# A fused linear-attention and MLP block: value products ahead of the key products, and a new hand-written order

## The chip, the cores and the metric

The kernel runs on one core of a Trainium2 chip. The core has a matrix engine (PE, with its own weight loads, PEld), a vector engine (DVE), a scalar engine for activations (ACT), GpSimd (POOL) and SyncE (SP), which only issues DMAs here. The metric is the device time in microseconds (us). A time is the median of some runs; one further execution was recorded by the profiler, and all views of the profile come from it.

## The reference, cut to what matters

```python
def _A_ref(x, wqkv, w_phi, wo):              # S = 2048 tokens, D = 640, H = 32 heads of 20
    q, k, v = split(x @ wqkv)
    pq = einsum("bhsd,hdf->bhsf", q, w_phi)
    pk = einsum("bhsd,hdf->bhsf", k, w_phi)
    phi_q = concat([softmax(pq), softmax(-pq)])      # over the 20 features of a head
    phi_k = concat([softmax(pk), softmax(-pk)])
    kv = einsum("bhsf,bhsd->bhfd", phi_k, v)
    z  = einsum("bhsf->bhf", phi_k)
    num = einsum("bhqf,bhfd->bhqd", phi_q, kv)
    den = einsum("bhqf,bhf->bhq", phi_q, z)[..., None] + 1e-6
    return (num / den) merged over heads @ wo
def _B_ref(x, w1, w2):                       # 640 -> 1728 -> 640
    return silu(x @ w1) @ w2

h  = x + _A_ref(layernorm(x), wqkv, w_phi, wo)
h2 = h + _B_ref(layernorm(h), w1, w2)
```

## The kernel before, in words

The 2048 tokens are 16 tiles of 128. Everything but the inputs and the result stays on the chip. The products accumulate in `mm`, which is the whole accumulator memory: eight banks of 128 x 512 f32.

The program is a list of words, `ORDER`. Each word calls a function `op_<name>` with the numbers behind the dots, and `@n` names the bank of `mm` that it starts in. Each engine carries out its own instructions in the order of the words, and waits by semaphores for what its operands and its bank need. No scheduler moves anything. A letter at a word's end picks the engine: `v` is DVE, `a` is ACT, `p` is POOL, `s` is SP (`q` and `b` split a tile between POOL and DVE). The words that matter here:

- Loads: `lx.a.b` tiles a to b of x (160 KB a tile), `lk.a.b` and `lv.a.b` pieces of the key weights wk and the value weights wv (160 KB for each 128 rows, five in all), `lp` w_phi, `lq.c` a part of the query weights, transposed by the DMA into the memory of wk, `lo`, `l1`, `l2`, `lh` the later weights.
- Layernorm of a tile t: `st.t` statistics on DVE (L267, L268), `rs` the reciprocal root (L272 on DVE for one tile, then a power on POOL, L275), `xn.t` the normalised tile (L291 on DVE, L296 on ACT). It is transposed by PE (`xt.t`, L302, five matmuls against the identity, and a copy `xc.t`) or by the DMA (`xd.t`, L309).
- Key weights folded with w_phi, so that one product gives pk: `wt.c` transposes a chunk of wk on PE (L316), `wc.c` copies it out (L166 or L168), `ph` multiplies w_phi by a mask that `mk` makes (L195), `fk.c` is the fold (L331, six matmuls) and `fc.c` copies it into Wfk. `gk` and `gc` do the same for the query weights.
- Products of a tile, ten matmuls of 128 x 320 (L364): `kp.t` with Wfk, `vp.t` with wv. `vc.t` copies v out of the accumulator.
- phi_k of a tile: `ke.t` the exponentials on ACT (L389), `kr.t` sums and reciprocals on DVE (L397, L400), `kn.t` the division on POOL (L407; with `q` or `b` DVE does a part, L411). `cc.t` adds the tile to kv (L420, 32 small matmuls).
- When kv is complete, `kc` and `km` bring it into the form for the queries. `mt` (with `mc`, a mask) prepares that.
- Queries, by groups of four tiles: `qp.g.i` products (L451), `qe.g.i` exponentials. Then for each tile `dp.t` multiplies with kv (L486, 40 small matmuls over four banks), `dw.t` and `dr.t` form num / den on DVE (L500 to L515), `do.t` finishes it on POOL or DVE (L521), `td.t` transposes by DMA, `op.t` is the product with wo (L548), `oa.t` adds x on DVE (L557).
- The MLP: `sq`, `sr`, `hn`, `hd` the second layernorm, `up.g.k` products with w1 (L627, L637), `ua` silu, `yp` and `yh` products with w2 (L673, L686), `yo` and `yz` the last addition and the store.
- `wm.n` is a dummy matmul of n columns on constants (L262) whose result nobody reads.

Before, PE starts with ten dummies while wk comes in. Then it transposes and folds the key weights (`wt`, `fk`), transposes tiles 0 and 1, and begins with `kp.0` and `kp.1`. The value weights are loaded after wk and tiles 2, 3 and 8 to 11; the first value product is the third projection. The function that all projections share is

```python
def proj(t, W):
    ps = mm2()
    for half in range(2):
        for c in range(C):
            nc.tensor.matmul(
                ps[:, half, 0:320], tok(XnT[t // GT], t)[:, c, :], W[:, c, half * 320 : (half + 1) * 320],
                start=(c == 0), stop=(c == C - 1),
            )
    return ps
```

Of the kernel before, what the change touches and what calls it, by code (L numbers as in the profile page):

```python
# [9 lines left out]
ALU = mybir.AluOpType  # L10
# [8 lines left out]
F32 = mybir.dt.float32  # L19
# [40 lines left out]
yp.3.0 ua.3.3 do.14.1.p td.14 up.3.2@4 ua.3.2 op.14@0 oa.14 yo.5 up.3.0@4 yo.3 up.3.6@0 yh.2.1@2,6 ua.3.0  # L60
ua.3.6 up.3.4@4 sq.14 sr.14 hn.14.a hd.14 yp.9.0 yp.9.1 yo.9 up.3.5@0 ua.3.5 up.3.1@6 yp.6.0@0 ua.3.4 ua.3.1
yp.12.0@4 yp.12.1 yp.10.1@6 yp.7.1 yp.7.0 yo.7 yp.6.1 yh.2.0@2 yo.6 yh.3.0 yp.8.0 yp.8.1 yo.8 up.4.2@0
ua.4.2 up.4.1@2 ua.4.1 yo.12 up.4.0@4 yp.11.0@0 ua.4.0 up.4.3@2 ua.4.3 yp.14.0@4 yp.15.1@2 yp.10.0 yo.10
yp.14.1 yp.15.0 yh.4.0 yo.15 yo.14 yh.3.1@6,7 yp.11.1 yo.11 yp.13.0 yz.13.0.s yp.13.1 yz.13.1.a
"""

@with_exitstack
def kernel(
# [30 lines left out]
    H0 = [(32 * r) // DH for r in range(C)]  # L99
# [9 lines left out]
    first = early.enter_context(tc.tile_pool(name="first", bufs=1, side="right"))  # L109
# [38 lines left out]
    maskR = first.tile([P, C, 3, 32], BF16, name="maskR")  # L148
# [12 lines left out]
    tl = {}  # L161
# [10 lines left out]
    def wk2():  # L172
        return late["work"]
# [17 lines left out]
            base=DH, pattern=[[6 * DH - 128, C], [DH, 8]], channel_multiplier=-1,  # L191
        )

    def op_ph():
        nc.vector.tensor_tensor(  # L195
            phb[:],
            phr[:].unsqueeze(2).to_broadcast([P, C, 8, DH]),
            mask5[:].unsqueeze(3).to_broadcast([P, C, 8, DH]),
            op=ALU.mult,
        )  # L200
# [2 lines left out]
        for vp in Vps:  # L203
            nc.gpsimd.memset(vp[:, :, DH : DH + 1], 1.0)

    def op_mc(r0):
        if r0 == 0:
            nc.gpsimd.memset(maskR[:], 1.0)
        m = maskR[:, r0::2, :, :]
        n, b0 = (C + 1 - r0) // 2, 32 * r0 - DH * H0[r0]  # L210
        nc.gpsimd.affine_select(
            out=m, in_=m, compare_op=ALU.is_ge, fill=0.0,
            base=b0, pattern=[[64 - 3 * DH, n], [-DH, 3], [1, 32]], channel_multiplier=0,
        )
        nc.gpsimd.affine_select(
            out=m, in_=m, compare_op=ALU.is_gt, fill=0.0,
            base=DH - b0, pattern=[[3 * DH - 64, n], [DH, 3], [-1, 32]], channel_multiplier=0,
        )

    def op_mt():  # L220
        nc.vector.transpose(
# [256 lines left out]
    def op_dp(t):  # L478
        g, i = t // GT, t % GT
        b = at.pop(0)  # L480
        ps = mm[:, b : b + 4, :]
        for s in range(2):
            for r in range(C):
                for k in range(4):
                    lo = 32 * k
                    nc.tensor.matmul(  # L486
                        ps[:, k, (8 * s + H0[r]) * 22 : (8 * s + H0[r] + NJ[r]) * 22],
                        EqT[g][lo : lo + 32, s, r, i * P : (i + 1) * P],
                        KVBD[lo : lo + 32, s, r, 0 : NJ[r], :].rearrange("p j c -> p (j c)"),
                        start=(s == 0 and r == 0),  # L490
                        stop=(s == 1 and r == C - 1),
                        skip_group_check=True,
                    )
        tl["dp", t] = [ps[:, :, 176 * s : 176 * (s + 1)].rearrange("p k (h c) -> p k h c", c=22) for s in range(2)]

    def op_dw(t, how="p"):
        A = tl["dp", t]
        first = A[0][:, :, :, 0:21]
# [3 lines left out]
        if how == "c":  # L502
            kept = wk2().tile([P, 4, 8, 21], F32, name="kept", bufs=1)
            nc.scalar.copy(kept[:], first)
            first = kept[:]
        u = wk2().tile([P, 4, 8, 21], F32, name="u", bufs=4)
        nc.vector.tensor_tensor(  # L507
            u[:], A[1][:, :, :, 0:21], w[:].unsqueeze(3).to_broadcast([P, 4, 8, 21]), op=ALU.mult,
        )
        nc.vector.tensor_tensor(u[:], u[:], first, op=ALU.add)  # L510
        tl["u", t] = u[:].rearrange("p (a k) h c -> p a (k h) c", a=2)

    def op_dr(t):
# [226 lines left out]
```

## Time and profile before

| what | us |
|---|---|
| median of three runs | 238.05 (237.7 to 238.34) |
| the profiled execution | 238.18 |
| its span in the profile | 236.4 |
| PE busy in the span | 230.5 |
| DVE busy | 134.1 |
| ACT busy | 115.1 |
| POOL busy | 93.0 |

The span reaches from the first to the last event that the profile has of the program; the 1.8 us more of the execution's own time lie around it. In the profile a line of the timeline or of the chain of waits gives start and duration in us, the engine, the line of the program (L364), the operation, the tile written and the tiles read, and how many equal instructions were merged (x20). What stands in brackets is the idle time of the engine just before, and what ended it. The chain of waits is followed back from the last instruction. The ends of matmuls are modelled: in the timeline the last one of a row reaches some 0.15 us into the next row, in the chain the rows follow each other. Half of the page is a strip of 40 slices of the span (5.9 us each) with the busy share in tenths.

### The profile page before, as it was taken

What the parts mean: (1) busy time and instruction counts of PE and PEld (TensorE: products, weight loads), DVE (VectorE), ACT (ScalarE), POOL (GpSimd) and SP (SyncE); (2) the same over time, 40 slices, a digit from 0 to 9 for tenths busy, and PEclk for the clock granted to TensorE, in tenths of its full rate; (3) what the DMA queues carried; (4) which work ended last, traced back from release to release, by engine and by line L of the source; (5) the groups of instructions that cost most, each with busy time, mean ns of one, the idle gap of its engine ahead of it and who ended that gap; (6) DMA issues with size and microseconds to landing.
All of it is one profiled execution on the core that took longest, in us unless ns stands there. A gap on an engine that the chain in (4) does not pass through costs nothing.

```text
span 236.4 us, 6319 instructions
## 1 busy us (share of the span) xinstructions
PE 230.5 (97%) x2672; PEld 147.5 (62%) x2672; DVE 134.1 (57%) x257; ACT 115.1 (49%) x172; POOL 93.0 (39%) x184
## 2 busy tenths in 40 slices
PE   7999999999999999999999999999999999999994
PEld 3777777677544455886755545556654657687762
DVE  3999999899848989989886504321203100220131
ACT  3898999856966575663055244644024250013000
POOL 7486897798913444187071600533000100000000
PEclk9999999999999999999999999999999999999999
DMA  7965778594001849123734501113311100020012
GB/s 209 297 249 113 109 121 180 140 265 141 3 6 34 179 81 197 34 55 61 111 86 90 99 10 28 29 30 57 83 30 55 28 28 3 28 86 0 0 65 76
DMA packets 44844, 20.67 MB, mean 87 GB/s; under 512 B 34448, under 2 KB 44304, under 8 KB 44816
## 3 DMA queue, kind: packets, MB, share of 16 engines
q1 hardware_dynamic: 43728, 19.88, 36.8%
q10 hardware_dynamic: 1088, 0.39, 0.7%
q8 instruction: 21, 0.34, 0.6%
q14 instruction: 7, 0.06, 0.1%
HBM read 9.61 MB, written 2.62 MB: 52 GB/s over the span
## 4 chain that ended last, share of the span: by engine, by line
PE 92%; DVE 2%; DMA 2%; ACT 1%; issue 0%; ACTq 0%; DVEq 0%
PE mm L627 24%; PE mm L673 24%; PE mm L364 19%; PE mm L548 9%; PE mm L451 7%; PE mm L486 3%; PE mm L420 2%; DMA wk<-in_A_wqkv_dram 2%; PE mm L331 2%; ACT EqT L461 1%; PE mm L637 1%; PE mm L686 1%; DVE u L507 1%; DVE u L510 1%; PE mm L302 1%; PE mm L316 1%
## 5 line engine op out<-in xcount | busy, mean ns | idle before, releaser
L627 PE MATMUL mm<-HnT,w 128*128 128x512 bf16 (+1 forms) x325 | 59.1, 337 | 0.0
L649 ACT ACTIVATE shT<-mm 128x1024 bf16<-128x1024 f32 (+2 forms) x29 | 27.7, 964 | 63.7 <-PE mm L627 48.2
L673 PE MATMUL mm<-w,shT 128*128 128x320 bf16 (+2 forms) x416 | 58.5, 299 | 0.0
L673 PEld LDWEIGHTS <-shT 128*128 128x128 bf16 x416 | 39.8, 98 | 17.7 <-issue 0.8
L627 PEld LDWEIGHTS <-w 128*128 128x128 bf16 x325 | 31.3, 98 | 22.8 <-issue 0.3
L694 DVE TENSOR_TENSOR ob<-mm,X 128x640 bf16<-128x640 f32 x15 | 12.0, 818 | 47.0 <-PE mm L673 29.4
L364 PEld LDWEIGHTS <-XnT 128*128 128x128 bf16 x320 | 30.7, 98 | 12.1 <-issue 0.3
L407 POOL TENSOR_TENSOR Ek<-Ek,Sk 128x1280 bf16<-128x1280 bf16 (+2 forms) x16 | 34.6, 2184 | 3.2 <-DVE Sk L400 3.2
L557 DVE SCALAR_TENSOR_TENSOR X<-mm,X 128x640 bf16<-128x640 f32 x16 | 13.1, 823 | 21.3 <-PE mm L548 21.1
L397 DVE TENSOR_REDUCE Sk<-Ek 128x64 f32<-128x1280 bf16 x16 | 23.3, 1455 | 1.6 <-ACT Ek L389 1.5
L548 PE MATMUL mm<-wo,ot 128*128 128x320 bf16 x160 | 23.9, 299 | 0.2 <-ACT EqT L461 0.2
L521 POOL TENSOR_TENSOR o<-u,rd 128x320 bf16<-128x320 f32 x20 | 14.6, 745 | 22.7 <-DVE rd L515 16.1
L364 PE MATMUL mm<-Wfk,XnT 128*128 128x320 bf16 x160 | 23.5, 299 | 0.0
L364 PE MATMUL mm<-wv,XnT 128*128 128x320 bf16 x160 | 23.4, 299 | 0.0
L451 PE MATMUL mm<-XnT,Wfq 128*128 128x512 bf16 x100 | 23.3, 380 | 0.0
L461 ACT ACTIVATE EqT<-mm 128x1024 bf16<-128x1024 f32 (+1 forms) x24 | 19.6, 884 | 7.5 <-PE mm L451 7.4
L389 ACT ACTIVATE Ek<-mm 128x640 bf16<-128x640 f32 x32 | 20.6, 710 | 2.8 <-PE mm L364 2.1
L548 PEld LDWEIGHTS <-ot 128*128 128x128 bf16 x160 | 15.4, 98 | 7.4 <-issue 0.7
L565 ACT ACTIVATE sq<-X 128x640 bf16<-128x640 bf16 x16 | 11.7, 731 | 9.3 <-DVE X L557 7.7
L267 DVE BATCH_NORM_STATS2 stats<-X 128x6 f32<-128x320 bf16 x32 | 13.7, 468 | 4.3 <-DMA X<-in_A_x_dram 4.3
L577 POOL TENSOR_SCALAR hm<-hst,hm 128x1 f32<-128x1 f32 x16 | 4.4, 273 | 28.0 <-ACT sq L565 27.0
L451 PEld LDWEIGHTS <-Wfq 128*128 128x128 bf16 x100 | 9.1, 98 | 9.9
(78 smaller groups left out, 215.2 us busy)
## 6 DMA issues: line engine op xcount, KB each, us to landing
out_dram<-ob SPq DMA_DIRECT2D x15, 160.0 KB, 1.8
w<-in_B_w_dram SPq DMA_DIRECT2D x6, 360.0 KB, 5.4
X<-in_A_x_dram SPq DMA_DIRECT2D x3, 640.0 KB, 6.9
w<-in_B_w_dram SPq DMA_DIRECT2D x5, 320.0 KB, 4.0
wk<-in_A_wqkv_dram SPq DMA_DIRECT2D x4, 160.0 KB, 3.7
wv<-in_A_wqkv_dram SPq DMA_DIRECT2D x1, 480.0 KB
wo<-in_A_wo_dram SPq DMA_DIRECT2D x1, 480.0 KB
w<-in_B_w_dram SPq DMA_DIRECT2D x1, 480.0 KB, 4.4
```

Source lines behind the costliest of these rows:

```text
L267: nc.vector.bn_stats(stats[:, k, :], X[:, t, k * 320 : (k + 1) * 320])
L364: nc.tensor.matmul(ps[:, half, 0:320], tok(XnT[t // GT], t)[:, c, :], W[:, c, half * 320 : (half + 1) * 320], start=(c == 0), stop=(c == C ...
L389: nc.scalar.activation(Ek[:, s, :].rearrange("p (a n) -> p a n", a=2), tl["kp", t][:, :, 0:320], AF.Exp, scale=1.0 - 2.0 * s,)
L397: nc.vector.tensor_reduce(Sk[:], tl["ek", t][:].rearrange("p s (h f) -> p (s h) f", f=DH), axis=AX.X, op=ALU.add,)
L407: nc.gpsimd.tensor_tensor(Ek3[:, 0:n], Ek3[:, 0:n], Sk[:, 0:n].unsqueeze(2).to_broadcast([P, n, DH]), op=ALU.mult,)
L451: nc.tensor.matmul(ps[:, k, :], Wfq[:, c, r * P : (r + 1) * P], XnT[g][:, c, :], start=(c == 0), stop=(c == C - 1),)
L461: nc.scalar.activation(E[:, s, rs[0] : rs[-1] + 1, :], tl["qp", g, i][:, 0 : len(rs), :], AF.Exp, scale=1.0 - 2.0 * s,)
L521: (nc.vector if eng == "v" else nc.gpsimd).tensor_tensor(tl["o", t][:, a * 320 : (a + 1) * 320].rearrange("p (h f) -> p h f", f=DH), tl["u ...
L548: nc.tensor.matmul(ps[:, half, 0:320], tl["ot", t][:, c, :], wo[:, c, half * 320 : (half + 1) * 320], start=(c == 0), stop=(c == C - 1),)
L627: nc.tensor.matmul(ps[:, i * W : (i + 1) * W], w1[:, c, fc * P : (fc + 1) * P], HnT[g][:, c, 0:W], start=(c == 0), stop=(c == C - 1), skip ...
L649: nc.scalar.activation(sh[:, a:b], tl["up", g, k][:, 0 : b - a], AF.Silu)
L673: nc.tensor.matmul(ps, shT[g][:, fc * W + i * P : fc * W + (i + 1) * P], w2[:, fc, a:b], start=first and fc == 0, stop=last and fc == FC - ...
```

## The change

The five weight pieces of wv are loaded first, together with tiles 0 to 3 of x; wk comes behind them. PE still starts with dummies, some more of them, and six more stand behind the first transposition `xt.0`. Then PE does `vp.0`, and the transpositions and folds of the key weights stand between `vp.0`, `vp.2`, `vp.3` and `vp.1`; `kp.2` is the first key product. The statistics of all tiles come before the first `kr`. `ph` moves from DVE to POOL, and the two halves of the mask `mc` become one word. All later words of all engines are in a new order too, with the same matmuls: among others the order of the tiles in `kp`, `vp`, `cc` and `dp`, the place of the loads `lo`, `l1`, `l2`, which engine does which `xn`, `hn` and `do`, and which `kn` are split (three by `b`, none by `q`; before, two and four). The branch `how == "c"` of `op_dw` is rewritten; no word of either order calls it.

The start of both orders, up to where the key products follow each other, and the stage from the last `cc` to `dp.9` or `dp.8`:

```diff
-lx.0.1.a lk.0.1.s lp.a lx.1.2.s lk.4.5.a lk.1.2.s lk.2.3.s lk.3.4.s mk mo wm.512@7 wm.512@7 wm.512@7
-wm.512@7 wm.512@7 wm.512@7 wm.512@7 wm.512@7 wm.512@7 wm.256@7 wt.0@0 st.0 rs.0.1 wm.256@2 wm.128@2 wt.4@1
-ph ta st.1 wc.0.a wt.1@2 lx.2.4.s wc.1.v fk.0@4 wt.2@3 wc.2.v lx.8.12.s wc.4.a fc.0.a fk.4@6 fc.4.a rs.1.2
-xn.0.v fk.1@0 fc.1.a wt.3@2 wc.3.v fk.2@4 fc.2.a xt.0@3 xn.1.v xc.0.v st.2 rs.2.3 mc.0 st.9 fk.3@6 fc.3.a
-xn.2.v xt.1@2 st.8 xc.1.a rs.8.10 kp.0@0 ke.0 kp.1@4 lv.0.3.s ke.1 lv.3.5.s xt.2@3 xc.2.a vp.1@6 lq.1.s st.3
...
+lx.0.1.a mo mk lx.2.4.s lv.0.2.s lx.1.2.a lv.2.4.s st.0 lp.a lv.4.5.s lk.0.1.s ta rs.0.1 xn.0.v lk.1.2.s
+st.2 rs.2.3 lk.2.4.s wm.512@7 wm.512@7 wm.512@7 wm.512@7 wm.512@7 wm.512@7 wm.512@7 wm.512@7 wm.512@7
+wm.256@7 wm.256@1 wm.256@1 wm.256@1 wm.128@1 xt.0@0 xc.0.a wm.256@1 wm.256@1 wm.256@1 wm.256@1 wm.256@1
+wm.256@1 vp.0@2 wt.0@1 st.3 rs.3.4 xn.2.v xt.2@4 wt.1@5 vc.0.a xn.3.v ph.p xt.3@6 st.1 rs.1.2 xc.2.a wc.0.a
+wc.1.a wt.3@7 wc.3.a lx.8.12.s wt.2@0 wc.2.v xn.1.v vp.2@2 vc.2.a lk.4.5.s lx.12.16.s xc.3.v fk.0@0 fc.0.v
+fk.3@4 fc.3.a mc st.9 st.8 st.15 rs.8.10 xt.1@7 xn.9.v xc.1.a wt.4@6 wc.4.a fk.2@2 fc.2.a vp.3@0 st.13
+fk.1@4 fc.1.a vc.3.a fk.4@6 fc.4.a xn.8.a st.12 rs.12.14 st.14 rs.14.16 lx.4.8.s vp.1@2 lo.2.5.s st.4 st.7
+st.6 rs.6.8 kp.2@4 xn.13.v ke.2 lq.2.s xd.9 vc.1.a st.5 kp.1@0 ke.1 kp.3@6 xn.12.a kp.0@4 ke.0 lo.0.2.s
...
-qe.0.0 qp.0.2@6 cc.7 close kc qe.0.2 qp.3.0@2 l2.4.6.s l2.6.8.s km.1 km.0 dp.0@4 dw.0.p dr.0 do.0.0.p l1.2.s
-l1.3.s qe.3.0 do.0.1.p qp.1.0@0 dp.1@2 qe.1.0 dw.1.p dr.1 do.1.1.p qp.1.1@6 dp.3@0 dw.3.p qe.1.1 do.1.0.v
-dr.3 do.3.0.p do.3.1.p qp.2.0@4 qe.2.0 dp.2@0 dw.2.p dr.2 qp.1.2@6 qe.1.2 td.0 do.2.0.p l1.4.s l1.5.s op.0@4
-do.2.1.p td.1 oa.0 td.3 dp.4@0 dw.4.p sq.0 sr.0 qp.2.1@6 qe.2.1 td.2 dr.4 qp.2.2@4 dp.6@0 hn.0.v hd.0 dw.6.p
-do.4.0.p qe.2.2 qp.3.2@5 op.1@6 qe.3.2 dp.5@0 oa.1 sq.1 l2.8.10.s l2.10.13.s op.2@4 qp.3.1@6 qe.3.1 dw.5.p
-do.4.1.p td.4 sr.1 dp.9@0 hn.1.v lh.s oa.2 dr.5 dw.9.p do.5.0.p sq.2 op.3@4 oa.3 do.5.1.p op.4@6 oa.4 dp.7@0
...
+qe.0.0 mt cc.5 close kc km.0 qe.0.2 qp.3.0@4 km.1 qe.3.0 dp.0@0 dw.0.p dr.0 do.0.1.p qp.1.1@6 qe.1.1 dp.3@0
+dw.3.p dr.3 do.0.0.p td.0 qp.2.0@4 qe.2.0 dp.1@0 dw.1.p qp.1.0@6 qe.1.0 qp.1.2@4 qe.1.2 dr.1 do.1.1.v dp.2@0
+do.3.1.p dw.2.p dr.2 qp.2.2@5 l2.8.10.s do.3.0.p op.0@6 oa.0 qe.2.2 do.1.0.p do.2.1.p sq.0 do.2.0.p dp.4@0
+td.3 l1.2.s dw.4.p dr.4 qp.2.1@4 qe.2.1 td.1 op.1@6 l1.0.s sr.0 dp.6@0 qp.3.2@4 do.4.1.p do.4.0.p oa.1 sq.1
+hn.0.a sr.1 dw.6.p qe.3.2 dr.6 do.6.1.p hn.1.v op.3@6 l1.3.s oa.3 l1.1.s dp.5@0 dw.5.p dr.5 do.5.1.p
+qp.3.1@4 qe.3.1 l2.0.2.s td.2 op.2@6 oa.2 sq.2 dp.9@0 sq.3 do.5.0.p dw.9.p td.4 op.4@4 oa.4 hd.0 hd.1 dr.9
+do.9.0.v up.0.0@6 ua.0.0 dp.7@0 dw.7.p l2.2.4.s l2.4.6.s dr.7 sr.2 do.6.0.p sq.4 up.0.1@4 ua.0.1 up.0.3@6
+do.9.1.p ua.0.3 dp.8@0 dw.8.p dr.8 td.5 op.5@4 sr.3 up.0.2@6 oa.5 td.6 dp.13@0 dw.13.p hn.3.a hd.3 op.6@4
...
-    def op_ph():
-        nc.vector.tensor_tensor(
+    def op_ph(eng="v"):
+        (nc.vector if eng == "v" else nc.gpsimd).tensor_tensor(
```

In the value-first order wv stands ahead of wk in SP's queue, the order of the last words is `... yp.13.0 yz.13.0.s yp.13.1 yz.13.1.a` in both, and the words between the two cuts hold the remaining `kp`, `vp`, `gk`, `cc` and their helpers.

More of the change, by code (lines that the diff above doesn't have):

```diff
@@ L204, in op_mo, with op_mc @@
             nc.gpsimd.memset(vp[:, :, DH : DH + 1], 1.0)
[L206 to L218, printed above, removed]
+    def op_mc():
+        nc.gpsimd.memset(maskR[:], 1.0)
+        for r0 in range(2):
+            m = maskR[:, r0::2, :, :]
+            n, b0 = (C + 1 - r0) // 2, 32 * r0 - DH * H0[r0]
+            nc.gpsimd.affine_select(
+                out=m, in_=m, compare_op=ALU.is_ge, fill=0.0,
+                base=b0, pattern=[[64 - 3 * DH, n], [-DH, 3], [1, 32]], channel_multiplier=0,
+            )
+            nc.gpsimd.affine_select(
+                out=m, in_=m, compare_op=ALU.is_gt, fill=0.0,
+                base=DH - b0, pattern=[[3 * DH - 64, n], [DH, 3], [-1, 32]], channel_multiplier=0,
+            )
     def op_mt():
@@ L497, in op_dw @@
         A = tl["dp", t]
-        first = A[0][:, :, :, 0:21]
+        if how == "c":
+            kept = wk2().tile([P, 4, 352], F32, name="kept", bufs=1)
+            nc.scalar.copy(kept[:], tl["ps", t])
+            A = [kept[:, :, 176 * s : 176 * (s + 1)].rearrange("p k (h c) -> p k h c", c=22) for s in range(2)]
         w = sm.tile([P, 4, 8], F32, name="w")
@@ L509, in op_dw @@
         )
[L510 removed]
+        nc.vector.tensor_tensor(u[:], u[:], A[0][:, :, :, 0:21], op=ALU.add)
         tl["u", t] = u[:].rearrange("p (a k) h c -> p a (k h) c", a=2)
```

57 lines of the change are left out of this document (25 added, 32 removed).

## The prediction

> **What bounds the kernel now.** I read the page first, then who waited for whom on PE, then PE's part of the timeline for the first 13 us, then all engines there, then the chain of waits.
>
> ```profile
> PE 230.5 (97%) x2672; PEld 147.5 (62%) x2672; DVE 134.1 (57%) x257; ACT 115.1 (49%) x172; POOL 93.0 (39%) x184
> ...
> PE   7999999999999999999999999999999999999994
> ...
> DVE  3999999899848989989886504321203100220131
> ```
>
> PE is busy in every slice but the first and the last. DVE is nearly full too, until about slice 20 (118 us). The waits of PE (total us, times, longest):
>
> ```profile
> PE mm L316 <- DMA wk<-in_A_wqkv_dram: 0.9, 1, 0.9
> PE mm L486 <- DVE u L510: 0.8, 3, 0.4
> PE mm L262 <- PEq L724: 0.8, 1, 0.8
> PE mm L548 <- ACT EqT L461: 0.2, 1, 0.2
> ```
>
> So a change of order can win only at the start and in the stage where L486 (the `dp` products) waits for DVE. After that PE waits for nothing. PE's timeline (start, us):
>
> ```profile
> 0.83 3.69 PE L262 MATMUL mm<-const-bfloat16-1.0 128*128 128x512 bf16 x10 [0.83 <-PEq L724]
> ...
> 5.88 0.73 PE L316 MATMUL mm<-ident,wk 128*128 128x128 bf16 x10 [0.91 <-DMA wk<-in_A_wqkv_dram]
> 6.45 0.48 PE L331 MATMUL mm<-phb,wTk 128*128 128x140 bf16 x6
> ...
> 9.74 2.98 PE L364 MATMUL mm<-Wfk,XnT 128*128 128x320 bf16 x20
> ```
>
> L262 is dummy work. By 9.79 (the chain's start of L364) PE has done five transposed weight chunks (`wt`, 0.28 each in the chain), five folds (`fk`, 0.32) and two token transposes (`xt`, 0.28): 1.40 + 1.60 + 0.56 = 3.56 us. From there the pieces of the chain follow each other, 1.36 a projection (20 matmuls 2.72). So the start has cost PE 9.79 - 3.56 = **6.23 us** in which it did nothing useful. Since the total PE work is the same in both kernels, this number, plus later losses, is what the change moves.
>
> **The change part by part.**
>
> *The first product.* A value product needs wv and normalised, transposed tokens; the old fold needs neither. The path of tile 0 in the timeline of all engines:
>
> ```profile
> 3.94 0.89 DVE L267 BATCH_NORM_STATS2 stats<-X 128x6 f32<-128x320 bf16 x2 [3.94 <-DMA X<-in_A_x_dram]
> ...
> 5.10 0.15 DVE L272 TENSOR_SCALAR RS<-MV 128x1 f32<-128x1 f32 x1
> 5.19 0.99 DVE L195 TENSOR_TENSOR phb<-phr,mask 128x800 bf16<-128x800 bf16 x1
> 5.34 1.24 POOL L275 TENSOR_TENSOR RS<-RS,nhalf 128x1 f32<-128x1 f32 x1 [0.85 <-DVE RS L272]
> ...
> 7.95 0.44 DVE L291 TENSOR_SCALAR xn<-X,MV,RS 128x640 bf16<-128x640 bf16 x1
> ```
>
> Tile 0 is still first in ACT's queue (before, it landed 3.1 after its issue). SP's first load beside it is now 320 KB instead of 160; if the queues are served in turn, that changes nothing for the first 160, so I keep 3.94. Statistics and L272 end at 5.25. The power on POOL took 1.24 here, and 0.67, 0.55 and 0.54 the three other times with one column; I take 0.6, as DVE's L195 is no longer beside it: 5.95. `xn.0` 0.44: 6.45. `xt.0` then starts at 6.51 and ends, as the trace models ends, 0.45 later; ACT's copy 0.70 is over at 7.70 and `vp.0` starts at **7.75**. Bounds: 6.4 if X lands in 1.8 us (what a 160 KB output takes, alone), 8.4 if the power takes 1.24; I stay by the row of X itself. Is wv there? By 5.88 the DMA had moved 209 GB/s x 5.88 = 1.23 MB; from 5.88 to 9.79 it moved 322 GB/s. Tiles 0 to 3, phi and wv are 1.5 MB: landed at about 6.8, inside the cover. PE has then done one `xt`: 7.75 - 0.28 = 7.47, **1.24 worse** than 6.23. The eight extra dummies, six of them behind `xt.0` (6 x 0.107 = 0.64, to 7.45), fall in time in which PE would wait.
>
> [...] Were the 1.24 instead the price of a first power, the sum below would be 0.65 higher.
>
> *Products with the folds between them.* I laid the new order on the engines with these durations: DVE has `xn.0` to 6.45, statistics of tile 2 (1.13) and tile 3 (1.15) with their L272, `xn.2` to 9.42, `xn.3` (its power ends 9.7) to 10.2, tile 1's statistics to 11.45, `wc.2` to 11.95. PE: `vp.0` to 9.11, `wt.0` to 9.39, waits 0.1 for `xn.2`, `xt.2`, `wt.1`, waits 0.2 for `xn.3`, `xt.3`, `wt.3`, `wt.2` to 11.1, `vp.2` to 12.46, two folds to 13.1. The mask product (`ph`) is now POOL's, not shown there: 0.99 on DVE below, 2.40 (L407, 1280 elements) above; I take 1.8 (L407 with 960), so 10.1 to 11.9, under the cover of `vp.2` (gone above 2.3). Behind it on POOL stands tile 1's power, to 12.55, and behind that on DVE `xn.1` (13.05), `xc.3` (13.5), `fc.0` (14.25). So `wt.4` (bank of `xt.3`) and `vp.3` (bank of `fk.0`) wait about 0.15 each. ACT's copies (0.65 apart) stay ahead. `kp.2` starts at 17.66, after 4 x 0.28 + 5 x 0.28 + 5 x 0.32 + 4 x 1.36 = 9.56 of work: 17.66 - 9.56 = **8.10**, 1.87 worse than 6.23. With the bounds of the first product and early waits between 0.2 and 1.2 the start is 0.1 to 3.1 worse.
>
> wk comes behind wv, three pieces and the last behind tiles 8 to 11: 0.66 and 0.16 MB more at 322 GB/s give about 9 and 11.5 us, ahead of `wt.2` (10.8) and `wt.4` (13.5): no cost. On SP, `lq.2` waits for `wt.4` (13.8) and then issues 1.3 us; `xd.9` behind it needs `xn.9` only at about 17.8: no cost.
>
> *The key chain.* Statistics now all stand ahead of the first `kr` on DVE: 14.25 + 12 x 1.0 + 4 x 0.4 = 27.9 (before 22.0). `kr` takes 1.95, so POOL's first `kn` starts at about 29.9 instead of 24.2, with no `rs` left between: 13 x 2.36 + 3 x 1.86 = 36.3, to 66.2; the last `kr` gets its exponential at about 61 and stretches this to some 66 to 67. PE reaches the last `cc` at 66.26 + 1.87 = 68.1. Cover 1 to 2 us: cost 0. (Before, POOL ended at 66.02, cover 0.24.)
>
> *The stage of `dp`.* Here DVE is late:
>
> ```profile
> 68.83 0.46 PE mm L486 x40
> ...
> 70.18 0.87 DVE u L507
> 71.05 0.02 issue
> 71.07 0.86 DVE u L510
> 71.94 0.04 issue
> 71.98 0.51 PE mm L486 x34
> ```
>
> A `dp` waits until DVE has emptied its banks, 2.65 after the last one ended; PE has 2.16 of `qp` meanwhile. From 68.83 to `dp.7` (95.53) PE has 65 x 0.216 + 5 x 1.36 + 8 x 0.40 = 24.0 of work in 26.7: 2.65 lost, some 0.9 of it hand-overs that stay. The new order has 2.16, 2.16, 3.24, 2.44, 3.52, 2.44, 3.52, 3.54 of PE work between the same eight; against DVE's `dw` 2.4, `dr` 0.35, `oa` 0.83 in their new order I find 0.59, 0.46, 0.15, 0.26, 0.15, 0.46, 0.1, 0.15 lost, 2.3 in all, and 0.2 at `dp.8`. Gain about 0.2; bounds -0.8 to +1.75. On SP, `td.2` now stands behind `l1.2`, `l1.0`, `l1.3`, `l1.1` and `l2.0.2` (1.8 MB, at 322 GB/s about 5.5 us from `dp.0` + 10 on); it lands near `dp.0` + 18 to 20, and `op.2` asks at + 23: 0. Behind that PE has far more work than DVE in both orders, and the end (two `yz`) is the same: 0. The joined `mc` has the same five POOL instructions, in POOL's idle time before 24; the rewritten branch of `op_dw` is called by neither order: 0.
>
> Sum against the profiled execution (238.18 = span 236.4 + 1.8 around it; 0.13 above the median): 238.18 + 1.24 + 0.63 - 0.2 = 239.85, so **239.9**.
>
> **The rivals.**
> 1. *The `dp` waits go* (the other side). If the longer stretches of `qp` hide the emptying everywhere, the 1.75 that are not hand-overs come back: 238.18 + 1.87 - 1.75 = 238.3. For: three stretches of over 3.2. Against: two of 2.16 stand first, as before. It decides when `dp.0` to `dp.7`, less `up.0.0` (2.18), is under 25.5 (before 26.7, forecast 26.35). With a start at its better bound it would be faster, 236.6 at the least.
> 2. *The key chain is late.* With `kn` at its longest, 2.60, POOL's sum is 39.4 and its end 69.3, past 68.1; with waits for late exponentials 1.2 to 2.2, on the forecast's 239.9: 241.6. It decides when PE waits for POOL at the last `cc`. For: `kr` starts six us later. Against: the sum above.
> 3. *PE's clock falls back.* PE idles from about 4.8 to 6.5 and is thin until 7.75. The dummies came 0.43 apart at first (weight loads at 1.64, 2.06, 2.49, 2.92), 512 columns later took 0.216. Slow for another 3 us, PE loses 1.5: 241.4. Against: the 0.91 wait at 5.88 left five transposes at 0.28.
>
> [...]
>
> **How the numbers follow.** Forecast 0.5 (239.1 to 240.8), rival 1 0.21, rival 2 0.2, rival 3 0.09. Slower by over 0.3% (0.7 us, about what a measurement of this kernel can tell from no change) is the forecast and rivals 2 and 3: 0.79. Rival 1 gives 0.15 within and 0.06 faster. The range leaves out rival 1 where a better start comes to it, and the worst of rival 2: 238.1 to 242.3.
>
> **What would show it.** Right: first L364 near 7.75, on wv; first L364 on Wfk near 17.7; L195's place on POOL at 1.5 to 2.3; first L407 near 30; PE waiting for no POOL before `dp.0`; `dp.0` near 70.5; the three to four waits on DVE u still there. Wrong: X landing under 3 us, a first L364 before 7, `dp` waits gone, PE waiting on DMA wv or wk, or dummies and transposes at twice their time behind 6 us.

## The result, and the profile after

The changed kernel takes 239.81 us in the median of four runs (239.65, 239.73, 239.88 and one of 242.24), the kernel before 237.9 beside it (237.7 to 238.34, four runs). The ratio is 1.0088, with a 95% interval of 1.006 to 1.0117: slower by some 0.9%. In a second comparison (`e11_after_again` below) the ratio was 1.0096 (1.0073 to 1.012). Three of its six runs (240.99 to 241.19) were lengthened by a fall of PE's clock (a mean granted clock of 0.993), which is taken up below; the other three, 239.81 to 239.93 against 238.1, give 1.0072 to 1.0077. The profiled execution took 239.65, its span is 237.9.

From the page, PE's busy time and the strips of PE and of its clock:

```profile
PE 229.4 (96%) x2660; PEld 148.7 (63%) x2680; DVE 133.5 (56%) x249; ACT 115.6 (49%) x173; POOL 97.5 (41%) x189
...
PE   8799999999988999999999999999999999999995
...
PEclk9999999999999999999999999999999999999999
```

PE is full in the same way as before; the strip has a thin second slice (6 to 12 us). The waits of PE (total us, times, longest) name new places:

```profile
PE mm L303 <- POOL RS L278: 1.4, 1, 1.4
...
PE mm L487 <- DVE u L511: 0.7, 2, 0.5
...
PE mm L421 <- POOL Ek L408: 0.5, 1, 0.5
```

The wait for wk is gone. A wait of 1.4 ahead of `xt.0` stands in its place. The view names POOL's L278, which ended last; what `xt.0` reads is `xn.0`, which DVE finished at 7.07 behind POOL's root of tile 0. At L421 (`cc`) PE now waits for the last division of a key group, which it did not before. (All lines are one higher than before.) PE's timeline shows the start:

```profile
0.83 4.88 PE L263 MATMUL mm<-const-bfloat16-1.0 128*128 128x512 bf16 x14 [0.83 <-PEq L725]
7.12 0.45 PE L303 MATMUL mm<-ident,xn 128*128 128x128 bf16 x5 [1.41 <-POOL RS L278]
...
8.36 1.53 PE L365 MATMUL mm<-wv,XnT 128*128 128x320 bf16 x10
...
10.82 0.45 PE L303 MATMUL mm<-ident,xn 128*128 128x128 bf16 x5
...
17.87 2.34 PE L365 MATMUL mm<-Wfk,XnT 128*128 128x320 bf16 x16
```

The first value product starts at 8.36, the first key product at 17.87. By then PE has done 9.56 us of useful work, so 8.31 were lost; before, by the same view, 9.74 - 3.56 = 6.18. The start is **2.13 worse**. In the timeline of all engines, three rows say where my sizes were off or right:

```profile
4.64 0.89 DVE L268 BATCH_NORM_STATS2 stats<-X 128x6 f32<-128x320 bf16 x2 [4.64 <-DMA X<-in_A_x_dram]
...
6.04 0.54 POOL L276 TENSOR_TENSOR RS<-RS,nhalf 128x1 f32<-128x1 f32 x1 [1.67 <-DVE RS L273]
...
10.77 1.52 POOL L196 TENSOR_TENSOR phb<-phr,mask 128x800 bf16<-128x800 bf16 x1
```

Tile 0 landed at 4.64, not at 3.94. The power took 0.54. The mask product took 1.52 on POOL. The last row of POOL's timeline ahead of `dp.0`, and the last `cc` in PE's:

```profile
59.85 8.38 POOL L408 TENSOR_TENSOR Ek<-Ek,Sk 128x640 bf16<-128x640 bf16 x4 [0.71 <-DVE Sk L401]
```
```profile
68.28 0.37 PE L421 MATMUL mm<-Ek,Vp 128*21 128x40 bf16 x32 [0.54 <-POOL Ek L408]
```

POOL's last division ends at 68.24, and PE, done with the `cc` before it at 67.74, waits 0.54.

The 1.5 us of span then add up from the two timelines:

| stretch of PE | before | after | difference |
|---|---|---|---|
| lost ahead of the first key product | 6.18 | 8.31 | +2.13 |
| from there to the last `cc`, without the wait for POOL (useful work taken off) | 56.45 - 6.0 = 50.45 | 50.41 - 0.54 = 49.87 | -0.58 |
| the wait for POOL | 0 | 0.54 | +0.54 |
| last `cc` to the end of the last matmul | 167.13 | 166.88 | -0.25 |
| after the last matmul | 3.08 | 2.74 | -0.34 |

The 6.0 are the useful work that the new order does ahead of its first key product and the old one behind it (9.56 - 3.56). The last row is no gain of the new order: the other profiles have 2.7 to 2.9 there, `e1_newhead` with the old tail among them, and only this one of the kernel before has 3.1.

### The profile page after: what moved, and what is told of

It is laid out like the page before. It is cut to its first block, busy times and chain, and to the rows that moved or that the text cites. A ratio compares the mean times of both kernels' runs of the same rounds, so it can differ in the third digit from the quotient of the medians.

```text
span 237.9 us, 6297 instructions
## 1 busy us (share of the span) xinstructions
PE 229.4 (96%) x2660; PEld 148.7 (63%) x2680; DVE 133.5 (56%) x249; ACT 115.6 (49%) x173; POOL 97.5 (41%) x189
## 4 chain that ended last, share of the span: by engine, by line
PE 85%; DVE 5%; POOL 3%; ACT 2%; issue 2%; DMA 2%; DVEq 0%; POOLq 0%; ACTq 0%
PE mm L674 24%; PE mm L628 24%; PE mm L365 16%; PE mm L549 8%; PE mm L452 5%; PE mm L487 2%; POOL Ek L408 2%; ACT EqT L462 2%; DMA X<-in_A_x_dram 2%; PE mm L421 1%; PE mm L332 1%; PE mm L638 1%; PE mm L687 1%; DVE stats L268 1%; DVE u L508 1%
## 5 line engine op out<-in xcount | busy, mean ns | idle before, releaser
L628 PE MATMUL mm<-HnT,w 128*128 128x512 bf16 (+1 forms) x316 | 58.3, 335 | 0.5
L408 POOL TENSOR_TENSOR Ek<-Ek,Sk 128x1280 bf16<-128x1280 bf16 (+1 forms) x16 | 35.8, 2269 | 2.6 <-DVE Sk L401 2.6
L522 POOL TENSOR_TENSOR o<-u,rd 128x320 bf16<-128x320 f32 x23 | 18.0, 796 | 33.7 <-DVE rd L516 27.6
L452 PE MATMUL mm<-XnT,Wfq 128*128 128x512 bf16 x90 | 22.1, 379 | 1.2 <-issue 0.6
L508 DVE TENSOR_TENSOR u<-mm,w 128x672 f32<-128x672 f32 x16 | 13.7, 857 | 1.3 <-DVE w L506 0.3
```

Source lines behind the costliest of these rows:

```text
L408: nc.gpsimd.tensor_tensor(Ek3[:, 0:n], Ek3[:, 0:n], Sk[:, 0:n].unsqueeze(2).to_broadcast([P, n, DH]), op=ALU.mult,)
L452: nc.tensor.matmul(ps[:, k, :], Wfq[:, c, r * P : (r + 1) * P], XnT[g][:, c, :], start=(c == 0), stop=(c == C - 1),)
L522: (nc.vector if eng == "v" else nc.gpsimd).tensor_tensor(tl["o", t][:, a * 320 : (a + 1) * 320].rearrange("p (h f) -> p h f", f=DH), tl["u ...
L628: nc.tensor.matmul(ps[:, i * W : (i + 1) * W], w1[:, c, fc * P : (fc + 1) * P], HnT[g][:, c, 0:W], start=(c == 0), stop=(c == C - 1), skip ...
```

## The experiments

Where nothing else is said, an edit is to the changed kernel. The letters in the expectations: S, the loss arises at the start; L, it arises behind the keys; D, the longer rows of the load beside tile 0 delay its landing; F, a product that starts earlier is passed on to the end; V, VectorE's row of normalisations holds the start wherever the first product is; C, the clock; K, the key chain on GpSimd.

**Head and tail apart.** Two kernels join one order up to the word `close` (where kv is complete) with the other behind it. The loads that both halves had, or neither, were set right.

```diff
-qe.0.1 qe.0.0 mt cc.5 close kc km.0 qe.0.2 qp.3.0@4 km.1 qe.3.0 dp.0@0 dw.0.p
+qe.0.1 qe.0.0 mt cc.5 close kc qe.0.2 qp.3.0@2 l2.4.6.s l2.6.8.s km.1 km.0 dp.0@4 dw.0.p
```

> The new order up to the word `close` (start, key and value products, kv), the old order behind it; the loads that the two parts would share are put where the old order has them. Theory S (the loss is made at the start, where PE begins its useful work some 2.1 us later, and is carried to the end because PE is full from there on): 239.6 to 240.3, like the changed kernel's 239.8 or up to 0.4 above it, because the old stage of `dp` is kept. Theory L (the loss is made behind `close`, by the new order of `dp`, MLP and loads): 237.7 to 238.5, like the kernel before.

Measured: 241.57 (240.14 to 241.93), ratio 1.0132 (1.0107 to 1.0157). The spread of 1.8 is taken up below, under the clock: four of the five runs have the fall (a mean granted clock of 0.993), and the profiled execution, 240.14 (0.999), has not.

```diff
-qe.0.0 qp.0.2@6 cc.7 close kc qe.0.2 qp.3.0@2 l2.4.6.s l2.6.8.s km.1 km.0 dp.0@4 dw.0.p
+qe.0.0 qp.0.2@6 cc.7 close kc km.0 qe.0.2 qp.3.0@4 km.1 qe.3.0 dp.0@0 dw.0.p
```

> The mirror image: the old order up to `close`, the new one behind it. Theory S: 237.4 to 238.1, as the kernel before or up to 0.4 under it, since from `dp.0` to the last product the new order took 164.3 us in the trace and the old one 164.5. Theory L: 239.3 to 240.0, like the changed kernel.

Measured (an edit to the kernel before): 237.85 (237.49 to 238.48, 11 runs), ratio 0.9987 (0.9976 to 0.9997). So the whole loss is in the new head, and the new tail is worth about 0.3. PE's waits with the old head hold the old entry for wk and none for POOL:

```profile
PE mm L318 <- DMA wk<-in_A_wqkv_dram: 0.8, 1, 0.8
PE mm L488 <- DVE u L512: 0.7, 2, 0.5
```

**What sets the start.** First, tiles 2 and 3 are loaded by two DMAs of 160 KB, the second of them behind the first part of wv, so that tile 0 has a small load beside it, as before:

```diff
-lx.0.1.a mo mk lx.2.4.s lv.0.2.s lx.1.2.a lv.2.4.s
+lx.0.1.a mo mk lx.2.3.s lv.0.2.s lx.1.2.a lx.3.4.s lv.2.4.s
```

> The changed kernel with tiles 2 and 3 of x loaded by two DMAs of 160 KB instead of one of 320, the second behind the first two pieces of wv. Tile 0 landed at 4.64 in the changed kernel and at 3.94 before. Theory D (the queue beside it, with one row of 2560 bytes for each of 1280, takes two thirds of the engines' time): tile 0 lands at about 3.9 to 4.1, `vp.0` starts at 7.6 to 7.8 instead of 8.36, and the time falls by 0.5 to 0.8, to 239.0 to 239.3. Rival (the number of bytes or of queues in flight decides, not the row): it lands at 4.5 to 4.7 and the time stays at 239.6 to 240.0.

Measured: 239.26 (239.2 to 239.66), ratio 1.0049 (1.0034 to 1.0063). Tile 0 landed at 4.05, as theory D had it (the edit changes the bytes and the row length of the load together, so which of the two counts is not shown; the two thirds of D were my estimate from the row lengths, and no run shows them). The first value product started at 7.78 (7.75 had been forecast). PE's timeline behind it:

```profile
7.78 1.53 PE L367 MATMUL mm<-wv,XnT 128*128 128x320 bf16 x10
...
11.00 0.73 PE L319 MATMUL mm<-ident,wk 128*128 128x128 bf16 x10 [0.31 <-DMA wk<-in_A_wqkv_dram]
...
17.78 2.47 PE L367 MATMUL mm<-Wfk,XnT 128*128 128x320 bf16 x17
```

0.58 earlier at the first product is 0.09 at the first key product in this execution, because PE waits for a piece of wk that lands at 10.95. This limit is not one of the changed kernel: by the landings in its trace the same piece arrived at 9.64 there, ahead of its use at 11.11, and in none of the ten profiles with the 320 KB load does PE's list of waits name wk. Three of the five runs were at 239.2, some 0.6 under the changed kernel, the profiled one at 239.66. That these three had the early tile without the late piece would fit, but the one trace can't show it.

Next, tile 0 goes into `xt.0` as it was loaded (its normalisation is left out of the computation):

```diff
-            nc.tensor.transpose(ps[:, c, :], tl["xn", t][:, c * P : (c + 1) * P], ident[:])
+            src = X[:, 0, c * P : (c + 1) * P] if t == 0 else tl["xn", t][:, c * P : (c + 1) * P]
+            nc.tensor.transpose(ps[:, c, :], src, ident[:])
```

> The changed kernel, but `xt.0` transposes tile 0 of x itself and not its normalised copy, so tile 0 isn't normalised for its products; the statistics and `xn.0` are still computed on DVE. PE can then start `vp.0` about 2 us earlier, once wv has landed. Theory F (the path of tile 0 to the first product alone sets the start): `vp.0` at 6.3 to 6.9 and the time falls by 1.3 to 2.0, to 237.8 to 238.5. Theory V (DVE's own row of statistics, tile 0, 2, 3, ahead of `xn.3` is a second path of the same length): `vp.0` comes earlier, but PE then waits before `xt.2` and `xt.3`, which stay at 9.9 and 10.8, and the time falls by 0 to 0.4.

Measured: 239.87 (239.58 to 239.93), ratio 1.0069 (1.0055 to 1.0084); no change. The timeline of PE shows the gain being given back:

```profile
6.31 0.43 PE L368 MATMUL mm<-wv,XnT 128*128 128x320 bf16 x2 [0.60 <-DMA wv<-in_A_wqkv_dram]
7.64 1.30 PE L368 MATMUL mm<-wv,XnT 128*128 128x320 bf16 x8 [0.90 <-DMA wv<-in_A_wqkv_dram]
...
9.85 0.45 PE L306 MATMUL mm<-ident,xn 128*128 128x128 bf16 x5 [0.63 <-DVE xn L294]
...
10.74 0.45 PE L306 MATMUL mm<-ident,xn 128*128 128x128 bf16 x5 [0.15 <-DVE xn L294]
...
17.79 2.47 PE L368 MATMUL mm<-Wfk,XnT 128*128 128x320 bf16 x17
```

A first product two us earlier waits for wv (until 7.64) and then for `xn.2` and `xn.3`. `xt.3` starts at 10.74 instead of 10.82 and the first key product at 17.79 instead of 17.87, both 0.08 earlier, and tile 0 landed 0.08 earlier in this execution (4.56). So the edit itself gained nothing: F is out, V holds. The chain of waits of the changed kernel shows the row of DVE, from tile 0's landing through the statistics of tiles 2 and 3 and POOL's root of tile 3 to `xt.3`; behind that, PE works without a wait up to the first key product:

```profile
4.64 0.90 DVE stats L268 x2
...
7.06 0.81 DVE stats L268 x2
...
8.29 0.81 DVE stats L268 x2
...
9.60 0.69 POOL RS L276
...
10.31 0.46 DVE xn L292
...
10.82 0.45 PE mm L303 x5
```

Since the row begins with the landing, executions must be compared from there. The changed kernel, `e1_newhead`, `e5_raw0`, `e9_fill` and `e10_fill_kn7` have tile 0 at 4.56 to 4.83 and the first key product 13.23 or 13.24 behind it, all five.

If V holds, work taken off DVE there should help and work added should hurt. The mask product goes back to DVE:

```diff
-xn.3.v ph.p xt.3@6
+xn.3.v ph.v xt.3@6
```

> The changed kernel with `ph` back on DVE, at the same place in the order. POOL took 1.52 for it, DVE 0.99 before. DVE's row is then longer by 0.99 before tile 1's statistics, while the power behind it on POOL comes sooner. Theory V (DVE's row is one of the paths that set the start): `wc.2`, `xn.1`, `xc.3`, `fc.0` come 0.4 to 0.7 later, PE waits there for `wt.4` or `vp.3`, and the time rises by 0.2 to 0.6, to 240.0 to 240.4. Rival (it has cover): 239.6 to 240.0.

Measured: 240.72 (240.67 to 241.53), ratio 1.0106 (1.0083 to 1.0128). This was another chip than that of the runs above; against the kernel before on the same chip (238.26) it is 2.46 slower, where the changed kernel was 1.91 slower, and 1.71 in its later runs without the fall of the clock: 0.5 to 0.8 worse. In PE's timeline the folds wait for a copy that stands behind the mask product on DVE, and the first key product is 0.85 later. Of this, 0.19 is tile 0's landing (4.83 in this execution), and 0.66 the longer row:

```profile
13.55 0.79 PE L334 MATMUL mm<-phb,wTk 128*128 128x140 bf16 x12 [0.18 <-DVE wTk L169]
...
18.72 1.52 PE L367 MATMUL mm<-Wfk,XnT 128*128 128x320 bf16 x10
```

And the other way round: tiles 0, 2 and 3 are all transposed as loaded (their normalisation is left out), so that `xt.0`, `xt.2` and `xt.3` on PE no longer wait for DVE's row.

```diff
-            nc.tensor.transpose(ps[:, c, :], tl["xn", t][:, c * P : (c + 1) * P], ident[:])
+            src = X[:, t, c * P : (c + 1) * P] if t in (0, 2, 3) else tl["xn", t][:, c * P : (c + 1) * P]
+            nc.tensor.transpose(ps[:, c, :], src, ident[:])
```

> Tiles 0, 2 and 3 are transposed as they were loaded: their normalisation is left out of the computation. If VectorE's row of statistics (tiles 0, 2, 3) is what holds the first key product: xt.2 and xt.3 begin with their landings, kp.2 comes 0.3 to 0.8 earlier than 17.87, and the time is 238.9 to 239.4. If the landing of the weights near 11 us holds the row at the same place: kp.2 0 to 0.3 earlier, a wait of TensorE for a DMA in its place, and 239.4 to 240.0. If the key chain on GpSimd sets the end of this part: kp.2 earlier, but the last kn near 68.2 as before, and the time 239.6 to 240.0.

Measured: 239.76 (239.24 to 239.87, four runs), ratio 1.0063 (1.0044 to 1.0082). The profiled execution is the 239.24; the other three are where the changed kernel is. Its timeline of PE:

```profile
10.19 1.52 PE L368 MATMUL mm<-wv,XnT 128*128 128x320 bf16 x10
...
12.21 0.79 PE L335 MATMUL mm<-phb,wTk 128*128 128x140 bf16 x12 [0.51 <-DVE wTk L169]
...
17.46 2.74 PE L368 MATMUL mm<-Wfk,XnT 128*128 128x320 bf16 x19
```

`vp.2` starts 1.47 earlier than in the changed kernel (10.19, was 11.66), and the first key product 0.41 earlier (17.46). But tile 0 landed at 4.30 in this execution, 0.34 earlier: the first key product stands 13.16 behind it, only 0.07 less than 13.23. No weight is late. DVE's row is as long as before, and PE now waits for its next piece, the copy `wc.2` behind tile 1's statistics:

```profile
10.34 0.88 DVE L270 BATCH_NORM_STATS2 stats<-X 128x6 f32<-128x320 bf16 x2
...
11.58 0.49 DVE L169 COPY wTk<-mm 128x640 bf16<-128x640 bf16 x1
```

So V holds with a longer row than I had: DVE's work from the landing of tile 0 to the copies behind tile 1's statistics, with POOL's roots in it. Work on PE that no longer waits for parts of the row gains nothing or nearly so (`e5_raw0`, `e12_raw_all`), and a longer row costs (`e4_ph_dve`). A shorter row was not tried.

**The clock.** Without the six dummies behind `xt.0`:

```diff
-xt.0@0 xc.0.a wm.256@1 wm.256@1 wm.256@1 wm.256@1 wm.256@1 wm.256@1 vp.0@2
+xt.0@0 xc.0.a vp.0@2
```

> The changed kernel without the six dummies behind `xt.0`. PE then does nothing but five transpositions (0.28 us) from about 5.2 to 8.4 us. Theory C (such a thin stretch slows PE's clock, and the dummies prevent it): the ten matmuls of `vp.0` and those behind them take 0.27 each instead of 0.136 for some 3 us, and the time rises by 1 to 2, to 241 to 242. Theory S (the dummies only fill idle time): `vp.0` takes 1.36 as before, and 239.6 to 240.0.

Measured, on the chip of `e4_ph_dve`: 241.19 (240.85 to 242.69), ratio 1.013 (1.01 to 1.0159). All four executions had a mean granted clock of 0.993. (The profiled one, 242.69, also had a wait of 0.9 of PE for a tile transposed by DMA; its reason stays open.) The changed kernel itself was then run again, and beside it a kernel with 17 more dummies in the thin places:

```diff
+wm.256@1 wm.256@1 wm.256@1 wm.256@1 wm.256@1 wm.256@1 wm.256@1
+wm.256@1 wm.256@1 wm.256@1 wm.256@1 wm.256@1 wm.256@1 wm.256@1
 xt.0@0 xc.0.a wm.256@1 wm.256@1 wm.256@1 wm.256@1 wm.256@1 wm.256@1
+wm.256@1 wm.256@1 wm.256@1
 vp.0@2
```

> The changed kernel again, without an edit, so that the two kernels beside it have it on the same chip. Theory C (in some executions the granted clock falls to 0.5 for one stretch of 3.4 us behind TensorE's thin stretch near 7 to 9 us, as two earlier runs show it): single runs either near 239.7 or 1.1 to 2.5 higher, and in a profile with a low run a 7 in the second slice of PEclk. Without C: all runs 239.5 to 239.9. Median 239.6 to 240.3 by both.

> Seventeen more dummy products of 256 columns in the gaps of TensorE's queue ahead of xt.0 and vp.0, so that it has no thin stretch. Theory C: the clock is 1.00 in every slice of the profile, the runs lie within 239.5 to 239.9, and the median is that of the changed kernel beside it or lower. Rival (the dummies are themselves in the way, since each takes 0.43 us while the array is still slow): xt.0 begins up to 0.3 later, and the time is 239.9 to 240.2.

Measured on one chip: the changed kernel 239.81, 239.81, 239.93 and 240.99, 241.03, 241.19. The first three had a mean clock of 1.0, the others 0.993. With the dummies: 239.79 to 239.94, clock 0.998 to 1.0, six runs of six. The profile of the changed kernel caught a drop; from its page:

```profile
PEclk9799999999999999999999999999999999999999
```

The same execution in stretches of a us (length, busy us of PE, PEld, DVE, ACT and POOL, then the granted clock, DMA share, GB/s):

```profile
7.00:8.00 1.00, 0.63 (x6) 0.63 (x7) 1.00 (x3) 0.00 (x0) 0.36 (x1) 0.70 1.07 344
8.00:9.00 1.00, 1.00 (x7) 0.69 (x6) 0.93 (x5) 0.69 (x1) 0.38 (x1) 0.50 1.14 398
9.00:10.00 1.00, 1.00 (x6) 0.59 (x5) 0.93 (x4) 0.00 (x0) 0.58 (x3) 0.50 1.02 407
10.00:11.00 1.00, 1.00 (x6) 0.61 (x5) 0.56 (x3) 0.00 (x0) 0.90 (x2) 0.59 1.04 396
```

At half speed for 0.60 + 1 + 1 + 0.82 = 3.42 us, from 7.40 to 10.82 (3.41 in the trace's record of the clock). Its first value product takes 2.34 instead of 1.53:

```profile
0.83 4.15 PE L265 MATMUL mm<-const-bfloat16-1.0 128*128 128x512 bf16 x14 [0.83 <-PEq L727]
7.37 0.72 PE L305 MATMUL mm<-ident,xn 128*128 128x128 bf16 x5 [2.39 <-POOL RS L280]
...
9.16 2.34 PE L367 MATMUL mm<-wv,XnT 128*128 128x320 bf16 x10
```

The first dummies are slow too, 0.43 apart. In this execution they came at full speed from 4.0 on and were done at 4.98; in the profiled execution of the first comparison the slow ones lasted longer, and the row of dummies reached 5.71. That, and tile 0 landing at 4.89 instead of 4.64, is why the wait ahead of `xt.0` was 1.41 there and 2.39 here. The trace's record of the granted clock begins where the array gets its full speed: in the kernel before at 3.86, where the weight loads of the dummies go from 0.43 apart to 0.21. Here it begins at 3.99, and 3.99 + 3.41 = 7.40: the fall came 3.41 us behind that. The moment differs between executions (3.45 to 6.78). PE's busy time in the 3.41 us behind it, by the view of stretches, in thirteen profiled executions (the trace of the fourteenth, `e8_oldhead_wk1`, has no record of the clock):

| execution of | stretch | PE busy in it | clock behind it |
|---|---|---|---|
| `e11_after_again` | 3.99 to 7.40 | 1.02 | 0.5 for 3.41 us |
| `e6_nodummy` | 6.00 to 9.41 | 1.33 | 0.5 for 3.41 us |
| `e7_kn7early` | 5.35 to 8.76 | 1.64 | 0.5 for 3.41 us |
| `e3_x2small` | 3.82 to 7.23 | 1.78 | 1.0 |
| the changed kernel | 5.50 to 8.91 | 1.88 | 1.0 |
| `e1_newhead` | 5.97 to 9.38 | 2.00 | 1.0 |
| `e4_ph_dve` | 6.26 to 9.67 | 2.24 | 1.0 |
| the kernel before | 3.86 to 7.27 | 2.50 | 1.0 |
| `e2_oldhead` | 4.32 to 7.73 | 2.60 | 1.0 |
| `e5_raw0` | 3.45 to 6.86 | 2.69 | 1.0 |
| `e9_fill` | 4.38 to 7.79 | 2.89 | 1.0 |
| `e10_fill_kn7`, `e12_raw_all` | 5.98 to 9.39, 6.78 to 10.19 | 3.41 | 1.0 |

The two groups do not overlap: with up to 1.64 of 3.41 (48%) the clock fell, with 1.78 (52%) and more it stayed. The ends of matmuls are modelled, so the shares are not exact to these few per cent. Two later places agree. In the 3.41 us that follow in `e5_raw0` (6.86 to 10.28) PE is busy for 2.01 (59%), and the clock stayed. At the end it fell in the kernel before at 235.96, behind 3.41 us with 0.78 of work (23%), and in the changed kernel at 237.61, behind 0.97 (28%). In the two profiles of the changed kernel PE was busy at the start for 1.02 us of the stretch (from 3.99) and for 1.88 (from 5.50); in the first the clock fell, in the second it stayed. So one kernel has both, and the execution decides. With the dummies PE was busy for 2.89 of it (`e9_fill`):

```profile
0.83 5.92 PE L266 MATMUL mm<-const-bfloat16-1.0 128*128 128x512 bf16 x28 [0.83 <-PEq L728]
7.27 0.45 PE L306 MATMUL mm<-ident,xn 128*128 128x128 bf16 x5 [0.52 <-POOL RS L281]
```

They are not in the way either: `xt.0` starts 2.49 behind tile 0's landing (4.78), in the changed kernel 2.48. In the slow part a dummy of 256 columns takes 0.21 (in `e10_fill_kn7` they start at 4.62, 4.83, 5.05), not the 0.43 of the expectation.

Over all runs: kernels with the new head and its late first product had the drop (a mean clock of 0.993) in 3 of 10 (the changed kernel), 4 of 5 (`e1_newhead`), 1 of 4 (`e4_ph_dve`), 2 of 4 (`e7_kn7early`, below), 4 of 4 (`e6_nodummy`); those with the dummies in 0 of 12; those whose `xt.0` starts by 6.6 (`e3_x2small`, `e5_raw0`, `e12_raw_all`) in 0 of 13; kernels with the old head never. The one run of 242.24 had a clock of 1.0: this is not its cause, and I don't know what was.

**The key chain.** `kn.7` goes ahead of `kn.11` on GpSimd, so that the last tile's division doesn't wait behind it; first alone, then in the kernel with the dummies:

```diff
-kp.6@2 kn.11.p lq.3.s
+kp.6@2 kn.7.p kn.11.p lq.3.s
...
-cc.6 kn.7.p cc.15
+cc.6 cc.15
```

> The changed kernel with one word moved: `kn.7.p` stands ahead of `kn.11.p`. In the changed kernel POOL idled 1.49 us before `kn.11` and 0.71 before `kn.6`, while the sums of tile 7 were ready, and its last `kn.5` ended at 68.24, with PE waiting 0.54 us for it. Theory K (a part of the loss is the key chain, late by that wait): POOL's last `kn` ends at 66.8 to 67.6, the wait of PE on POOL goes, and the time falls by 0.4 to 0.6, to 239.2 to 239.5. Theory S alone (only the start counts; the wait is replaced by another): 239.6 to 240.0.

Measured: 240.27 (240.04 to 240.58), ratio 1.008 (1.0059 to 1.01), with the drop of the clock in two of four runs, the profiled one among them. This was the chip of `e4_ph_dve`, with the kernel before at 238.26. PE's wait for POOL is gone from its trace, and from the first key product to `dp.0` it took 52.33 there (71.77 - 19.44), against 52.98 in the changed kernel (70.85 - 17.87); the median mixes runs with and without the drop.

> The filling dummies, and kn.7.p ahead of kn.11.p on GpSimd. Theory K (the wait of TensorE for the last key group's kn, 0.5 us, is a real part of the loss): 0.4 to 0.6 below the kernel with the dummies alone, 239.1 to 239.4, and no wait of TensorE for POOL behind the last products of the keys. Rival S (what is lost lies ahead of the first group of keys, and the wait is only its mirror): the same time as the kernel with the dummies alone, 239.5 to 239.9, and another wait in the same place.

Measured: 239.27 (239.17 to 239.47), ratio 1.0048 (1.0032 to 1.0063), beside 239.9 for the dummies alone on the same chip: **0.63 less**. POOL's last divisions and PE's last three `cc`, which now run through as one row:

```profile
63.30 4.17 POOL L411 TENSOR_TENSOR Ek<-Ek,Sk 128x1280 bf16<-128x1280 bf16 x2 [1.33 <-DVE Sk L404]
```
```profile
67.27 0.93 PE L424 MATMUL mm<-Ek,Vp 128*21 128x40 bf16 x96
```

`dp.0` starts at 70.39, with the dummies alone at 70.99, although tile 0 landed 0.05 later. So K holds: the wait is a real part of the loss. The two runs of `e7_kn7early` without a drop, 240.04 and 240.15, are 1.8 to 1.9 behind the kernel before on their chip, as the changed kernel is on its own, and don't show that gain; why is open.

**Better than before?** The old head with the new tail, and the second chunk of wk loaded ahead of tile 1 of x (an edit to `e2_oldhead`):

```diff
-lp.a lx.1.2.s lk.4.5.a lk.1.2.s lk.2.3.s
+lp.a lk.4.5.a lk.1.2.s lx.1.2.s lk.2.3.s
...
-wt.4@1 ph ta st.1 wc.0.a wt.1@2 lx.2.4.s
+wt.1@2 wt.4@1 ph ta st.1 wc.0.a lx.2.4.s
```

> The old order up to `close` and the new one behind it, which took 237.85 (0.9987 of the kernel before), and in the start the load of wk's second piece ahead of tile 1's and `wt.1` ahead of `wt.4`. PE waited 0.91 for wk before the two. If PE is limited there by what it can do before 5.9 us, `wt.1` moves into the wait, `kp.0` starts 0.2 to 0.3 earlier than 9.74, and the time is 237.5 to 237.7. If the copies and folds behind it are the limit (the mask product ends at 6.18 on DVE, and the folds wait for it), `kp.0` stays at 9.7 to 9.9 and the time at 237.7 to 238.1.

Measured: 237.96 (237.67 to 238.51, 12 runs), ratio 0.9984 (0.9973 to 0.9996), no different from `e2_oldhead` (0.9987). PE's wait for wk is gone from the trace, but the first key product stays at 9.93 behind a wait of 0.19 for a copy: the copies and folds are the limit there. These two are the fastest, 0.1 to 0.2% below the kernel before.

## Why the prediction was right, and where its steps were off

The time (239.9 against 239.81) and the mechanism, a dearer start that nothing behind it gives back, were right. Some terms were off and cancelled.

- *The first product, 1.24.* It cost 1.85: it started at 8.36, so 8.36 - 0.28 = 8.08 against 6.23. The step that failed is "that changes nothing for the first 160, so I keep 3.94": tile 0 landed at 4.64 beside a load of 320 KB (4.30 to 4.89 in ten profiles), and at 4.05 when that load was cut to 160 (`e3_x2small`). The path was off too. I let the first product carry the loss, but starting it 2 us earlier gained nothing (`e5_raw0`); the late landing counts because DVE's row begins with it. The power was right (0.6 taken, 0.54 measured). wv was still later than I had it (a part of it at 7.64 in `e5_raw0` and the last of it at 7.84 in the changed kernel, not all at 6.8), inside the cover.
- *Waits among the folds, 0.63.* They were 0.23 (9.51 from `vp.0` to `kp.2`, with 9.28 of work). The two terms together are 2.08 (8.31 - 6.23) for 1.87. That sum is luck: from tile 0's landing to the first key product I had 17.66 - 3.94 = 13.72, measured were 13.23, and these 0.49 paid for most of the 0.70 by which the landing was late. `vp.2` started at 11.66 where I had it at 11.1; the waits ahead of it were as forecast (0.25 for 0.3), and those of `wt.4` and `vp.3` behind it (0.3) did not come: ACT and DVE had 0.6 us more to be done with their copies. wk was right: I had it at about 9 and 11.5, its pieces landed at 8.29, 8.74, 9.64 and 11.67, ahead of their use.
- *The mask product on POOL, 0.* Right (1.52, 1.8 taken, under its cover of 2.3). On DVE it would have cost 0.66 at the first key product (`e4_ph_dve`).
- *The key chain, 0 with a cover of 1 to 2 us.* Wrong: it cost 0.54, and `e10_fill_kn7` gives 0.63 back. POOL's end at 68.24 is past my "66 to 67", although the first division started only 0.3 later than forecast (30.22 for 29.9): its own work was 35.8 (36.3 forecast), but two later divisions waited 1.49 and 0.71 for `kr`, where I had allowed 0.8 at most. This is rival 2, at the lower end of its condition and below its price of 1.2 to 2.2.
- *A term that I did not have:* -0.58 between the first key product and the last `cc`. The old order had small losses there that PE's list of waits does not show. Two make 0.46 of it: `xt.2` starts at 12.72, 0.26 behind the end of the first two key products, where the weight loads wait 0.33 for `xn.2`; and a row of 20 value products, 2.72 elsewhere, takes 2.92 (41.55 to 44.47). The second is not in the profile of `e2_oldhead`. That they pay for the key chain is luck.
- *The stage of `dp`, -0.2.* Right: -0.25 from the last `cc` to PE's end, and 0.3 by `e2_oldhead`. From `dp.0` to `dp.7`, less `up.0.0`, it was 26.4 (26.35 forecast). Rival 1, which needed 25.5, did not come.
- *Rival 3, the clock.* It came, but only in some executions, and not as I wrote it. Not the slow start lasts longer; a second slow stretch of 3.41 us begins in the thin part (7.40 to 10.82 in `e11_after_again`). Its price was 1.1 to 1.4 in `e11_after_again` (1.5 forecast). The stretches of 3.41 us ahead of the three falls were thin but not empty: PE was busy in them for 30 to 48%. The 0.09 that I gave it was an estimate: all that I had was one wait of 0.91 behind which the transposes ran at 0.28, and no run of a longer or thinner stretch. It is low beside 3 executions of 10.

## What to carry to other kernels

When a start is reordered, find the chain that holds its last common point, and not only the one to the first product: here the row on DVE held the first key product 13.2 us behind the landing of tile 0, whether the first value product started at 6.3 or at 8.6. Before two profiles are compared, take off what differs between executions of one kernel: with the same loads at the start, tile 0 landed anywhere between 4.30 and 4.89, and that alone was most of the gain that one trace seemed to show. Check the last member of each group in a chain that you count as covered, since 0.3 of delay at its start and a few waits inside used up a cover of 1 to 2 us. Where TensorE is thin for some 3 us, as here between 4 and 9 us, look at the granted clock of each run and not only of the profiled one, and try to fill the stretch: 17 dummies, with PE busy for 2.89 of 3.41 us, cost nothing here (239.9 against 239.81 to 239.93 at a clock of 1.0) and took out a difference of 1.2 us between executions.

## What the runs showed of the hardware

- At the start the granted clock fell to 0.5 for 3.41 us in three profiles, behind 3.41 us in which PE had been busy for 30% (`e11_after_again`), 39% (`e6_nodummy`) and 48% (`e7_kn7early`), and in none of ten others, where it had been busy for 52% or more. PE's wait ahead of `xt.0` was 2.39, 1.50 and 1.66 in the three; it was 1.63 in `e3_x2small`, which had 52% and kept the clock.
- Tile 0, a load of 160 KB, landed at 4.30 to 4.89 in ten profiles with a load of 320 KB issued beside it, at 4.05 in the one with 160 KB (`e3_x2small`), and at 3.84 to 4.05 in the three of the old head, where the load beside it is 160 KB of wk.
- A power with one column on POOL took 1.24 in the kernel before, where the mask product runs beside it on DVE (0.99 from 5.19). In the changed kernel it took 0.54 for tile 0, and 0.68 for tile 3, where it overlapped `xn.2` on DVE (0.44 from 9.43).
